# Reordering VectorE's queue in a fused mLSTM cell and gated feed-forward kernel

## The chip, the cores and the metric

The kernel runs on one core of a Trainium2 chip. A core has a matrix engine (TensorE, PE in the profile, its weight loads PEld), a vector engine (VectorE, DVE), an activation engine (ScalarE, ACT), a general engine (GpSimd, POOL) and a queue that here only issues transfers (SyncE, SP). Each engine works through its own instructions in order and waits on semaphores for the others. The metric is the device time of one execution in microseconds (us); less is better.

## The reference

For 4 batches, 8 heads, 768 steps and a head size of 40, an mLSTM cell is run step by step, its output becomes 3072 rows of 320, and a feed-forward block of width 2048 with the activation h * cos(h) follows:

```python
m_new = np.maximum(f_gate[:, :, t] + m, i_gate[:, :, t])
f_stab, i_stab = np.exp(f_gate[:, :, t] + m - m_new), np.exp(i_gate[:, :, t] - m_new)
C = f_stab[..., None, None] * C + i_stab[..., None, None] * np.einsum('bhd,bhe->bhde', vt, kt)
n = f_stab[..., None] * n + i_stab[..., None] * kt
denom = np.maximum(np.abs(np.einsum('bhd,bhd->bh', n, qt)[:, :, None]), 1.0)
y[:, :, t] = sigmoid(o_gate[:, :, t]) * np.einsum('bhde,bhe->bhd', C, qt) / denom
...
h = x @ w_in            # x: 3072 x 320, w_in: 320 x 2048
out = (h * np.cos(h)) @ w_out
```

w_in and w_out come as 64-bit floats and are made 32-bit on the chip.

## The kernel before, in words

**Chunks and periods.** The sequence is cut into 6 chunks c of 128 steps. One call of both_parts(c, b), called a *period* here, does the feed-forward of chunk c for a quarter of the width (two *slots*, each a pair of blocks of 128 columns of w_in for all four batches), and beside it the cell n = 4(c+1)+b, that is batch b of the next chunk. Chunk 5 has no cell beside it. first_cells does cells 0 to 3 ahead. Everything is emitted in one order written by hand (manual_schedule), and each engine's queue is that order cut down to its own instructions.

**A slot on the feed-forward side.** Up (L617) multiplies x by w_in into two PSUM tiles pup (L631 and L634, two buffers in all, so that the next Up waits until this one's are read). near (L639, ACT) rounds h to whole turns, rest (L642, DVE) forms the remainder, sin (L647, ACT) takes its sine, and gate (L654 in chunk 0, L659 in two halves after it, DVE) multiplies it with h: only the gate frees pup. sums (L723, POOL) forms sums of four blocks, and down or down_first (L727, L823, PE) multiply with w_out.

**The cell.** scores (L453, PE) writes ps. weigh (L459, DVE, two instructions) multiplies it into the decay matrix E in place and so frees ps. values_turned (L490 and L496, PE) writes hp into the PSUM buffers which ps had (pool ps_a has two), L496 with the weighed E. normalize_turned (L510 to L522, DVE) reads hp, fade (L577) decays the state, seam (L596, PE) makes the state's addition pu in a buffer that hp had, and state (L612, DVE) adds it. turn_blocks (L414) and turn_gates (L421, L425), on DVE, prepare the next cell. Cells below 7 (TURNED) use PE transposes and normalize instead.

**The decay matrix of the next cell** passes through three engines: decay_exponents subtracts on DVE (L375) and masks on POOL (L376), decay takes the exponential on ACT (L384). ACT changes its table for it and back for the sine (sin_next, L965), and then does the near of the second slot. On POOL the sums of the second slot stand behind the mask.

**Weights.** parts (ACT, L138 and L140) and join (DVE, L144, L146, L148, and an addition L149 on POOL, or on DVE where nc.vector is handed in) make 32-bit pieces. In chunk 0 a period makes three pieces of w_in for the next period (i=0 and i=1, 128x512, and w_in_l, 128x256) and two of w_out (128x640). The tiles wt and wm between parts and join have two buffers.

**Order of DVE in a period before.** First slot: rest, rest, weigh, in chunks 1 to 4 decay_exponents, gates; in chunk 0 the join of w_out and, after normalize, of w_in piece 1. Second slot: rest, rest, state, in chunk 0 the join of w_in piece 2, gates, in chunk 0 the join of w_in_l and of w_out, with turn_blocks and turn_gates between or after.

Of the kernel before, what the change touches and what calls it, by code (L numbers as in the profile page):

```python
# [29 lines left out]
def kernel(  # L30
# [20 lines left out]
    nc = tc.nc  # L51

    B, H, S, D = q.shape
# [16 lines left out]
    TURNED = 2 * B - 1  # L70
# [302 lines left out]
    def decay_exponents(n):  # L373
        E = Es[n]
        nc.vector.tensor_tensor(out=E, in0=E, in1=cols(n, 0, C), op=OP.subtract)  # L375
        nc.gpsimd.affine_select(out=E, in_=E, compare_op=OP.is_ge, fill=1.0e30, base=0,  # L376
                                pattern=[[0, H], [1, C]], channel_multiplier=-1)
# [461 lines left out]
    def first_cells():  # L839
        nc.vector.memset(nil, 0.0)  # L840
        gates_in()
        nc.scalar.copy(out=ident_b, in_=ident)
        load(0, "qk")
        later_gates_in()
        load(1, "qk")
        load(0, "v")
        load_o(0, (0, 1))
        load(2, "qk")
        load_E(0)
        load_E(1)  # L850
        warm(7)
        gates_first()
        later_fills()
        wall_in(0, 0, pmu)
        wall_in(0, 1, psum_o())
        spread(0, 0)
        gates_first_out()
        decay_exponents_half(0, 0)
        turn(0)
        turn_out(0, False)  # L860
        gates_sums()
        spread(0, 1)
        decay_exponents_half(0, 1)
        decay(0)
        weigh_k(0)
        load_E(2)
        load(1, "v")
        load(3, "qk")
        load(2, "v")
        load_E(3)  # L870
        load_o(0, (2, 3))
        load(3, "v")
        pieces.extend(weights_in(0))
        wall_in(1, 0, psum_o())
        wall_in(1, 1, psum_o())
        gates_less_sums()
        spread(1, 0)
        decay_exponents_half(1, 0)
        scores(0)
        gates_maxima()  # L880
        turn(1)
        weigh(0)
        turn_out(1, False)
        sigmoid(0, slice(0, 2))
        spread(1, 1)
        decay_exponents_half(1, 1)
        gates_exponents()
        decay(1)
        weigh_k(1)
        values(0)  # L890
        normalize(0)
        scores(1)
        turn(2)
        turn_out(2, False)
        warm(2)
        seam(0)
        weigh(1)
        seam_out(0)
        state(0)
        load_E(B)  # L900
        load(B, "qk")
        decay_exponents(2)
        decay(2)
        weigh_k(2)
        gates_exp()
        values(1)
        outs.append((0, weights_out(0)))
        load(B, "v")
        load_o(1, (0,))
        load_E(B + 1)  # L910
        normalize(1)
        scores(2)
        turn(3)
        seam(1)
        weigh(2)
        turn_out(3)
        seam_out(1)
        decay_exponents(3)
        gates_diagonal()
        values(2)  # L920
        decay(3)
        weigh_k(3)
        state(1)
        scores(3)
        weigh(3)
        pg = gates_turn()
        warm(5)
        values(3)
        join(*parts(*pieces.pop(0)))
        sigmoid(0, slice(2, 4))  # L930
        gates_keep(*pg)
        pieces.extend(weights_in(1))
        load(B + 1)
        outs.extend((p, weights_out(p)) for p in range(1, 3))
        load_o(1, (1, 2, 3))
        normalize(2)
        warm(5)
        seam(2)
        seam_out(2)
        second = parts(*pieces.pop(0))  # L940
        normalize(3)
        warm(4)
        seam(3)
        join(*second, nc.vector)
        decay_exponents(B)
        seam_out(3)
        join(*parts(*pieces.pop(0)), nc.vector)
        load_E(B + 2)
        state(2)
        state(3)  # L950

        nc.scalar.activation(out=spot, in_=spot, func=AF.Exp)
# [10 lines left out]
    def sin_next():  # L963

        nc.scalar.activation(out=spot, in_=spot, func=AF.Sin)  # L965
# [5 lines left out]
    def out_join(p, h, last=None):  # L971
        join(*h, last)
        if p + 3 < NF // 2:
            outs.append((p + 3, weights_out(p + 3)))

    def both_parts(c, b):

        n = (c + 1) * B + b
        cell = n < N
        begin = c == b == 0
        more = cell and n + 1 < N
        f2 = 2 * b
        slot = NF // 2 * c + f2
        sums(slot)
        up = Up(c, f2, cell_after_first if begin else None)
        if cell:
            scores(n)  # L990
            if begin:
                values_kept(n)

                warm(6, psum_o())
        for e in range(2):
            up.near(e)
        if begin:
            weigh(n)
        for e in range(2):
            up.rest(e)  # L1000
        if cell and not begin:
            weigh(n)
        if begin or more and c > 0:
            decay_exponents(n + 1)
        for e in range(2):
            up.sin(e)
            up.gate(e)
        if n == TURNED:
            turn_gates(n)
        if c == 0 and b == 1:  # L1010
            sigmoid(1, slice(1, B))
        if begin:
            sigmoid(1, slice(0, 1))
        h = ()
        if c == 0 and not begin:
            out_join(*out_parts())
        if pieces:
            h = parts(*pieces.pop(0))
        rests = []
        ends = any(step[2] == NP - 1 for step in plan.get(slot, ()))  # L1020
        if ends:
            rests = down(slot)
        if begin or more and c > 0:
            decay(n + 1)
        elif more:
            decay_by_bias(n + 1)
        if 0 < slot <= NP:
            down_first(slot - 1)
        elif slot and not ends:
            down(slot)  # L1030
        for rest in rests:
            rest()
        if cell:
            if n < TURNED:
                load(n + 2)
                if not begin:
                    values_kept(n)
                values(n)
                normalize(n)
                if h:  # L1040
                    join(*h)
            else:
                values_turned(n)
                if h:
                    join(*h)

                normalize_turned(n)
                if n + 2 < N:
                    load(n + 2, "q")
                last_in(n)  # L1050
                if n + 2 < N:
                    load(n + 2, "bkv")
            if TURNED <= n + 2 < N:
                load_G(n + 2)
            if n + 3 < N:
                load_E(n + 3)
            if b == B - 2 and c + 2 < NC:
                load_o(c + 2)
            fade(n)
            if n + 1 == TURNED:  # L1060
                turn_blocks(n + 1)
        h = ()
        sin_next()
        if pieces:
            h = parts(*pieces.pop(0))
        sums(slot + 1)
        up = Up(c, f2 + 1)
        if cell:
            seam(n)
        for e in range(2):  # L1070
            up.near(e)
        for e in range(2):
            up.rest(e)
        if cell and n < TURNED:
            seam_out(n)
        if cell:
            state(n)
        if h:
            join(*h)
        for e in range(2):  # L1080
            up.sin(e)
            up.gate(e)
        if b == B - 1 and 0 < c < NC - 2:
            sigmoid(c + 2)
            sin_next()
        if more:
            weigh_k(n + 1)
        if c == 1 and b < B - 1:
            two_differences(2 * b + 2)
        if pieces:  # L1090
            join(*parts(*pieces.pop(0)))
        if c == 0:
            down_first(f2)
        else:
            for rest in down(slot + 1):
                rest()
        if pieces:
            join(*parts(*pieces.pop(0)))
        if c == 0:
            if b + 2 < B:  # L1100
                pieces.extend(weights_in(b + 2))
            h = out_parts()
        if more and n + 1 < TURNED:
            turn(n + 1)
            turn_out(n + 1, c > 0)
        elif more and n + 1 > TURNED:
            turn_blocks(n + 1)
        if c == 0:
            out_join(*h)
            if b == B - 1:  # L1110
                more_units()
                two_differences(0)
                sigmoid(2)
                sin_next()
        if more and n + 1 > TURNED:
            turn_gates(n + 1)
# [43 lines left out]
```

## Time and profile before

| what | value |
|---|---|
| median of 5 runs | 535.59 us (533.8 to 539.48) |
| the profiled execution: its own time, its span | 535.59 us, 533.8 us |
| granted TensorE clock, mean | 0.997 |
| PE busy | 521.6 us (98%) |
| DVE busy | 397.3 us (74%) |
| ACT busy | 264.9 us (50%) |
| POOL busy | 209.8 us (39%) |

The span runs from the first to the last recorded instruction, and the time has 1.8 us around it. Chunk 0 begins at 37.6 us of the span, chunk 1 at 129.4, chunk 2 at 207.2, chunk 3 at 283.9, chunk 4 at 363.8 and chunk 5 at 442.6 (first Up of each). A timeline line gives start, duration, engine, line, operation and tiles, and in brackets the idle time before it with what ended it. A line of waits gives the total, the number and the longest.

### The profile page before, as it was taken

Reading aid. Unit: us, or ns where it says so; the run is one execution under the profiler, and the core shown is the slowest. Engines: PE = TensorE matmul, PEld = TensorE weight load, DVE = VectorE, ACT = ScalarE, POOL = GpSimd, SP = SyncE. Lnnn points to the kernel's source line nnn. Section 1 sums busy time; section 2 is a strip of 40 time slices with the busy share of each in tenths; the row PEclk is TensorE's granted clock in tenths of the full one; section 3 lists DMA queues with packets and bytes.
Section 4 is the critical chain, followed back from the end, with each engine's and each line's share of the span. In section 5 each row is a group of like instructions: output and inputs, shape, how many; then the busy total and the mean of one; then the engine's idle time right before and its main releaser. Section 6 shows DMA issues by size and latency. Waiting matters only on the chain.

```text
span 533.8 us, 10613 instructions
## 1 busy us (share of the span) xinstructions
PE 521.6 (98%) x3855; PEld 345.3 (65%) x3855; DVE 397.3 (74%) x864; ACT 264.9 (50%) x418; POOL 209.8 (39%) x409
## 2 busy tenths in 40 slices
PE   8999999999999999999999999999999999999996
PEld 6865566654565666556656567667567576657596
DVE  5779678889788887977988978968868854325253
ACT  4779696767633646552547353356354322313210
POOL 6423433333926531131531633533533425344350
PEclk9899999999999999999999999999999999999999
DMA  9999989822563365365266256266254100000000
GB/s 137 224 227 232 219 222 224 186 50 64 131 143 87 89 141 126 95 136 114 70 150 147 66 112 137 83 139 142 79 102 93 41 11 17 14 0 26 0 26 25
DMA packets 134860, 57.80 MB, mean 108 GB/s; under 512 B 70248, under 2 KB 130872, under 8 KB 134808
## 3 DMA queue, kind: packets, MB, share of 16 engines
q1 hardware_dynamic: 134664, 56.93, 48.2%
q8 instruction: 30, 0.49, 0.4%
q0 software_dynamic: 96, 0.18, 0.2%
q14 instruction: 22, 0.18, 0.1%
q10 hardware_dynamic: 48, 0.02, 0.0%
HBM read 50.76 MB, written 6.34 MB: 107 GB/s over the span
## 4 chain that ended last, share of the span: by engine, by line
PE 72%; DVE 12%; SPq 8%; DMA 3%; issue 2%; ACT 1%; POOL 1%; DVEq 0%; POOLq 0%; ACTq 0%
PE po L727 27%; PE pup L631 26%; PE pup L634 8%; PE po L823 4%; SPq L332 3%; PE ps L453 2%; PE hp L496 2%; DVE E L375 2%; DVE n L642 2%; DMA E<-M_d 1%; DVE wt L148 1%; PE hp L490 1%; DVE wt L146 1%; PE pu L596 1%; DVE E L459 1%
## 5 line engine op out<-in xcount | busy, mean ns | idle before, releaser
L631 PE MATMUL pup<-xT,w_in_sb 128*128 128x512 f32 x384 | 175.2, 599 | 3.6 <-DVE g L654 1.6
L639 ACT ACTIVATE n<-pup 128x512 int32<-128x512 f32 x96 | 52.0, 593 | 179.7 <-PE pup L634 179.7
L642 DVE SCALAR_TENSOR_TENSOR n<-pup,n 128x512 f32<-128x512 f32 x96 | 61.8, 686 | 91.0 <-ACT n L639 90.8
L631 PEld LDWEIGHTS pup<-xT,w_in_sb 128*128 128x128 f32 x384 | 69.6, 190 | 77.4 <-issue 63.4
L376 POOL TENSOR_SCALAR_AFFINE_SELECT E<-E 128x1024 f32<-128x1024 f32 x19 | 20.8, 1094 | 131.0 <-DVE E L375 125.1
L727 PE MATMUL po<-T,sg 128*128 128x160 f32 x426 | 69.5, 299 | 0.0
L647 ACT ACTIVATE n<-n 128x512 f32<-128x512 f32 x96 | 58.9, 630 | 16.1 <-DVE n L642 16.1
L727 PEld LDWEIGHTS po<-T,sg 128*128 128x128 f32 x426 | 61.7, 190 | 0.0
L723 POOL TENSOR_TENSOR sg<-g 128x128 f32<-128x128 f32 x66 | 30.2, 458 | 63.3 <-PE po L727 44.3
L634 PE MATMUL pup<-xT,w_in_l 64*128 64x512 f32 x192 | 54.2, 641 | 0.6 <-DVE w_in_l L149 0.6
L723 POOL TENSOR_TENSOR sg<-gg 128x128 f32<-128x128 f32 x66 | 30.2, 457 | 39.1 <-PE po L727 37.0
L634 PEld LDWEIGHTS pup<-xT,w_in_l 64*128 64x128 f32 x192 | 14.4, 184 | 37.0 <-issue 34.1
L727 PE MATMUL po<-w_out_sb,g 128*128 128x160 f32 (+1 forms) x180 | 38.3, 341 | 0.0
L823 PE MATMUL po<-w_out_sb,g 128*128 128x320 f32 x128 | 36.6, 439 | 0.5 <-POOL w_out_sb L149 0.4
L727 PEld LDWEIGHTS po<-w_out_sb,g 128*128 128x128 f32 x180 | 27.8, 189 | 11.0 <-issue 6.8
L414 DVE STREAM_TRANSPOSE t<-qs 128x512 f32<-128x512 f32 x34 | 34.9, 1105 | 0.0
L384 ACT ACTIVATE E<-E 128x1024 f32<-128x1024 f32 x21 | 22.2, 1058 | 25.3 <-POOL E L376 21.2
L727 PE MATMUL po<-w_out_sb,gg 128*128 128x160 f32 (+1 forms) x168 | 34.0, 329 | 0.0
L459 DVE TENSOR_TENSOR E<-ps,E 128x512 f32<-128x512 f32 x48 | 30.7, 680 | 2.5 <-ACT E L384 2.1
L453 PEld LDWEIGHTS ps<-t,t 40*128 40x128 f32 (+1 forms) x384 | 25.7, 192 | 9.7 <-issue 9.2
L659 DVE SCALAR_TENSOR_TENSOR g<-pup,n 128x256 f32<-128x256 f32 x82 | 30.6, 416 | 1.1 <-issue 0.6
L727 PE MATMUL po<-w_out_sb,sg 128*128 128x160 f32 x142 | 30.9, 299 | 0.0
(171 smaller groups left out, 852.5 us busy)
## 6 DMA issues: line engine op xcount, KB each, us to landing
E<-M_d SPq DMA_DIRECT2D x22, 512.0 KB
bits<-in_moe_w_in_dram SPq DMA_DIRECT2D x40, 128.0 KB
bits<-in_moe_w_out_dram SPq DMA_DIRECT2D x8, 640.0 KB
room<-G_d SPq DMA_DIRECT2D x34, 128.0 KB
ks<-in_k_dram SPq DMA_DIRECT2D x24, 160.0 KB
vs<-in_v_dram SPq DMA_DIRECT2D x24, 160.0 KB
out_dram<-o SPq DMA_DIRECT2D x18, 160.0 KB
o<-in_o_gate_dram SPq DMA_DIRECT2D x68, 40.0 KB
```

The source lines that it names most:

```text
L414: nc.vector.transpose(out=dst.rearrange("r p (t x) -> r p x t", x=T4), in_=src.rearrange("r p (x d) -> r p x d", x=T4)[:, :, :, 0:32])
L453: nc.tensor.matmul(ps[j][:, p], kT[r, p], qT[r, p], start=True, stop=True)
L459: nc.vector.tensor_tensor(out=w, in0=pss[n][j], in1=w, op=OP.mult)
L631: nc.tensor.matmul(pu, w_in_sb[:, i, ts(block(f2, e), 128)], x(i), start=(i == 0), stop=False)
L634: nc.tensor.matmul(pu, w_in_l[r, f2], x(NK, r), start=False, stop=True)
L639: nc.scalar.activation(out=self.n[e], in_=self.pu[e], func=AF.Copy, bias=0.25)
L642: nc.vector.scalar_tensor_tensor(out=self.n[e].bitcast(FP), in0=self.pu[e], scalar=0.25, in1=self.n[e], op0=OP.add, op1=OP.subtract)
L647: nc.scalar.activation(out=r, in_=r, func=AF.Sin, scale=TWO_PI_DOWN)
L659: nc.vector.scalar_tensor_tensor(out=gs[c, f2, s][:, ts(e, W)], in0=self.pu[e][:, ts(s, W)], scalar=TWO_PI, in1=n[:, ts(s, W)], op0=OP.mul ...
L723: engine.tensor_tensor(out=S[:, i], in0=x, in1=y, op=op)
L727: nc.tensor.matmul(out, g, w, start=start, stop=stop, skip_group_check=True)
L823: nc.tensor.matmul(po[0][b], gs[0, f // 2, f % 2][:, ts(b, C)], w_out_sb[:, f], start=(f == 0), stop=(f == NF - 1))
```

## The change

In chunks 1 to 4, one weigh moves between the two remainders of the first slot, decay_exponents of the next cell moves behind the gates, and in the second slot state moves behind the gates (from cell 7 on). In chunk 0, each period makes parts for w_in pieces 1 and 2 and joins both in its middle, ahead of the second slot's remainders; the join between state and the gates goes; fade moves ahead of these joins; the last join of w_out of each period ends on DVE instead of POOL; turn_blocks of cell 7 moves behind the gates. In first_cells the join of w_in_l and decay_exponents(4) change places. No instruction is added or removed but for the engine of four additions (128x640, L149).

```diff
@@ first_cells
         join(*second, nc.vector)
-        decay_exponents(B)
         seam_out(3)
         join(*parts(*pieces.pop(0)), nc.vector)
+        decay_exponents(B)
@@ both_parts
         if begin:
             weigh(n)
-        for e in range(2):
-            up.rest(e)
-        if cell and not begin:
+        up.rest(0)
+        if cell and c > 0:
             weigh(n)
-        if begin or more and c > 0:
+        up.rest(1)
+        if c == 0 and not begin:
+            weigh(n)
+        if begin:
             decay_exponents(n + 1)
         for e in range(2):
             up.sin(e)
             up.gate(e)
+        if more and c > 0:
+            decay_exponents(n + 1)
...
         if pieces:
-            h = parts(*pieces.pop(0))
+            h = [parts(*pieces.pop(0)) for _ in range(2 if begin else 1)]
...
                 values(n)
                 normalize(n)
-                if h:
-                    join(*h)
+                fade(n)
             else:
                 values_turned(n)
-                if h:
-                    join(*h)
+            if h:
+                if not begin:
+                    sin_next()
+                    h.append(parts(*pieces.pop(0)))
+                for piece in h:
+                    join(*piece)
+            if n >= TURNED:
...
-            fade(n)
-            if n + 1 == TURNED:
-                turn_blocks(n + 1)
-        h = ()
-        sin_next()
-        if pieces:
-            h = parts(*pieces.pop(0))
+            if n >= TURNED:
+                fade(n)
+        if begin or not h:
+            sin_next()
...
-        if cell:
+        if cell and n < TURNED:
             state(n)
-        if h:
-            join(*h)
         for e in range(2):
             up.sin(e)
             up.gate(e)
+        if n >= TURNED and cell:
+            state(n)
...
+        if n + 1 == TURNED:
+            turn_blocks(n + 1)
         if pieces:
             join(*parts(*pieces.pop(0)))
...
-        if pieces:
-            join(*parts(*pieces.pop(0)))
...
         if c == 0:
-            out_join(*h)
+            out_join(*h, nc.vector)
```

## The prediction

> **What bounds the kernel now.** I read the page's busy times first, then the waits of PE between 37 and 320 us, then the timeline of each engine over chunks 0 to 3.
>
> The busy times (us, share of the span, instructions):
>
> ```profile
> PE 521.6 (98%) x3855; PEld 345.3 (65%) x3855; DVE 397.3 (74%) x864; ACT 264.9 (50%) x418; POOL 209.8 (39%) x409
> ```
>
> PE sets the time. From the second period of chunk 3 on its timeline has no gap, so what other engines do there is worth nothing unless it becomes late. To be gained are PE's stalls before, and nothing more. Its waits (total us, number, longest):
>
> ```profile
> PE pup L631 <- DVE g L654: 1.6, 3, 0.6
> PE pup L631 <- DVE g L659: 0.9, 1, 0.9
> PE pup L634 <- DVE w_in_l L149: 0.6, 1, 0.6
> PE pu L596 <- DVE room L519: 0.5, 1, 0.5
> PE po L823 <- POOL w_out_sb L149: 0.4, 2, 0.2
> ```
>
> That is 4.0 us: mostly an Up that waits for gates, and pieces that are joined late. More hides in matmuls drawn long. PE in a chunk-1 period whose first slot has 16 w_out products of full width (L823, 4.5 us), and in one with 14 of half width (L727, 2.1 us):
>
> ```profile
> 139.40 0.67 PE L490 MATMUL hp<-room,st 40*32 40x128 f32 x32
> 141.01 3.70 PE L631 MATMUL pup<-xT,w_in_sb 128*128 128x512 f32 x8
> ...
> 157.87 0.94 PE L490 MATMUL hp<-room,st 40*32 40x128 f32 x32
> 159.95 3.70 PE L631 MATMUL pup<-xT,w_in_sb 128*128 128x512 f32 x8
> ```
>
> From hp's start to the next Up: 1.61 us in the first, 2.08 in the second. Seven periods are like the second (2.07 to 2.14). DVE says why:
>
> ```profile
> 155.61 1.29 DVE L642 SCALAR_TENSOR_TENSOR n<-pup,n 128x512 f32<-128x512 f32 x2 [2.17 <-ACT n L639]
> 156.82 1.28 DVE L459 TENSOR_TENSOR E<-ps,E 128x512 f32<-128x512 f32 x2
> 158.01 1.22 DVE L375 TENSOR_TENSOR E<-E,tab 128x1024 f32<-128x1024 f32 x1
> 159.14 1.41 DVE L659 SCALAR_TENSOR_TENSOR gg<-pup,n 128x256 f32<-128x256 f32 x4
> 160.47 0.51 DVE L510 STREAM_TRANSPOSE room<-hp 128x128 f32<-128x128 f32 x2
> ```
>
> hp is ready to start at 157.87, but the second weigh frees its buffer only at 158.10; the first gate's two halves end at about 159.9, where the Up starts. Weigh and gates are each late by less than a microsecond.
>
> **Chunks 1 to 4.** Let T be the start of the first remainder (155.61). Starts follow each other by 0.60 (L642, L459), 1.13 (L375) and 0.335 us (L659). New order: rest T, weigh T+0.60 and T+1.20, rest T+1.80. ACT's second sine (0.63 each) now starts after that, T+2.53 to T+3.16, so gate 0 runs T+2.40 to T+3.1 and gate 1 waits 0.13 and runs T+3.2 to T+3.9. L375 starts at T+3.87 (before T+2.40), L510 at T+5.0 (before T+4.86).
>
> Gain: the weigh ends 0.6 us earlier and gate 0 1.1 us earlier, more than the 0.5 us that PE loses there in all, so hp to Up becomes 1.61. In three periods of chunk 1 and two of chunk 2 (2.08, 2.13, 2.13, 2.14, 2.14) this gives 2.57. In the first periods of chunks 2 and 3 the half microsecond is lost again: PE then waits for L519 (at 221.74 and 298.88), which only gets later, by the 0.14 of L510; in chunk 3 also by POOL's later sums beside L521 to L577: I take -0.14 and -0.30. Bounds for the two together: 0 to -0.9 (three of those instructions stretched in each, as L577 was from 0.67 to 1.22 at 164.23).
>
> In the last period of chunk 2 the Up waits 0.9 at 283.87 for gates behind rest (281.15) and state (282.36). State goes behind them, 0.67. But ACT's near now ends its wait for the mask later: POOL's mask T+5.16, ACT's exponential T+6.3, table 1.28, dummy sine 0.2, near at 280.1 instead of 280.52 with PE 0.5 earlier. Up at 282.95 instead of 283.87, 0.92 of which 0.53 is counted above: 0.4 (0 to 0.6).
>
> The later mask is the new wait. Behind it on POOL stand the second slot's sums, 1.5 us later: at 240.0 rather than 238.5 for the first four against PE's use at 243.95, and in chunk 3 298.9 for the last four against about 302. Behind it on ACT stand the table, the dummy and near: 164.4 instead of 164.80, PE ready at about 164.15; DVE is not free before 165.9 in any case. State ends at 169.2; the scores that need its buffer start at 172.2. All hidden.
>
> **A rule against it.** POOL and DVE disturb each other:
>
> ```profile
> 120.81 1.24 DVE L512 SCALAR_TENSOR_TENSOR room<-room,least 128x8 f32<-128x8 f32 x1
> 122.09 1.01 DVE L513 SCALAR_TENSOR_TENSOR room<-room 128x8 f32<-128x8 f32 x1
> ```
>
> beside
>
> ```profile
> 120.50 1.53 POOL L149 TENSOR_TENSOR w_out_sb<-wt,wm 128x640 int32<-128x640 int32 x1 [6.79 <-ACT E L390]
> 121.98 1.09 POOL L391 TENSOR_SCALAR_AFFINE_SELECT E<-E 128x1024 f32<-128x1024 f32 x1
> ```
>
> Both end with the POOL instruction (L391 is the mask in chunk 0, of the same kind and length as L376); at 220.20 L512 took 0.17. The mask (1.09) used to lie under the gates, which read PSUM and kept their time; it now lies under L512 and moves everything up to L522 by 0.35 more. DVE's second remainders then start at 165.97 instead of 165.48, their gates at 167.2 against an Up at 168.7: hidden, and 1.4 us of DVE's 2.36 idle before the next period's remainder are left. The Trainium skill, "SBUF — State Buffer", Who interferes with whom, says that a DVE instruction with two SBUF inputs and a reading POOL instruction exclude each other for the whole instruction. By that rule L512 would be held for up to the whole mask, 1.09 per period, and by the rows for the 0.73 that is left of it at T+5.54. The gates' lead of 0.8 covers the 0.36 between them, so the sum is 3.97 by either.
>
> **Chunk 0.** (a) first_cells: w_in_l joined at 40.25 instead of 42.65 (the mask stretched its L146 to 1.08; its four steps unhindered, 0.33+0.3+0.43+0.43 from the nearest rows), so PE's 0.57 before L634 goes. Late next is weigh at 44.83, which stands behind the w_out join: that starts with ACT's L138 at 42.5 and meets kw on POOL. Gain 0.2 (-0.4 if kw holds a step for its 0.75, +0.4 if not). (b) Up at 60.78 and 107.93, each 0.63 idle, 0.80 late against the common step: the join between state and gates (0.43+0.43+0.69) goes, and w_in pieces come earlier. In the middle, the second join runs beside POOL's addition of the first (1.27) and takes about 2.5 instead of 1.6; fade (2 x 0.5 on POOL), now ahead of these additions, meets normalize's last steps and may cost up to 0.5 more, which is in the ends below. At 60.78 DVE had 2.55 idle there: gates at 58.1 instead of 59.95, PE ready at 59.9, gain 0.8. PE's wait for w_out at 66.62 (0.14 over the common step) goes, since DVE adds it in about 0.83 (0.69 x 640/512, L149 at 38.09) and not 1.54. (c) At 84.50 nothing was lost; rest moves from 79.90 to 81.3, gates stay at 83.2 to 84.4: 0. (d) At 107.93 DVE had no idle time. Gates at 106.3, so the Up starts at 107.13, but turn_blocks (2.1) now stands between the gates and the join of w_in_l, whose POOL addition ends at 111.1 to 111.6; L634 wants it at 110.6 and started at 111.53 before. Of 0.8, plus 0.28 for w_out at 113.77, I keep 0.3 (-0.1 to 1.1: the two ends of that join). Each w_out addition (0.83) on DVE ends before the next remainder, which had 1.29, 1.43, 1.29 and 0.85 idle.
>
> ACT's order: at the start of chunk 0 the second parts (1.2) go ahead of the exponential, same sum before near. The weights' transfers land early enough (4096-byte packets of w_in end at 44, 70 and 90 us against uses after 50, 78 and 99); SP issues in the same order.
>
> **Sum.** 2.57 - 0.44 + 0.4 + 0.2 + 0.8 + 0.14 + 0.3 = 3.97. The profiled execution took 535.59, which is also the median of the five runs: 535.59 - 4.0 = **531.6 us**, 0.7% less. Adding the low ends (five hp periods 1.8, -0.9, 0, -0.4, 0.6 for (b), -0.1) gives 1.0, the high ends (2.6, 0, 0.6, 0.4, 0.94, 1.1) 5.6: 530.0 to 534.6.
>
> **Rivals.** (1) All stalls go and DVE isn't held by POOL: high ends, and the waits at L596 (298.88) and 49.10 (0.5 each) too: 6.6, 529.0. For it: PE's remaining stalls are that small. Against: L519 gets later in my order. (2) The stalls go but come back at the next DVE wait (L634, L596, L519), or hp waits for turn_gates and not weigh: only (b) and 0.1 to 0.5 remain, 534.5. (3) Slower: the mask's place. If mask, exponential and two tables take over 1.8 us longer than I lay out (1.0 of DVE's own lateness and 0.8 of the gates' lead), the second slot's gates hold the Up in up to 15 periods; at 2.5 us it is 15 x 0.7 = 10.5, less 4: 542. Against: the chain's parts are measured (1.09, 1.06, 1.28, 0.2) and POOL is idle before the mask.
>
> **How the numbers follow.** A change of under about 1% can't be told from none in this kernel. Forecast 0.55, rival 1 0.20, rival 2 0.15, rival 3 0.10. Faster by over 1% is below 530.2: rival 1 and a little of the forecast, 0.23. Slower by over 1% (above 540.9): 0.08 of rival 3. Within 1%: 0.69. Range 528.8 to 536.5: it takes in the bounds, rival 2, most of rival 1 and rival 3's mild end.
>
> **What would show it.** L490's 32 at 0.67 and 1.61 from hp to Up in all periods of chunks 1 to 3; no wait before the second period's Up (60.78); a longer wait at L596 in the first periods of chunks 2 and 3; L512 near 0.7 under the mask; L634 near 111 waiting for POOL's w_in_l. Wrong if PE waits for g L659 in second slots (rival 3), or if L490 keeps 0.94.

## The result and the profile after

The changed kernel took 533.72 us (median of 45 executions, 531.69 to 536.76) against 534.6 (87 executions, 532.54 to 539.59) for the kernel before: a ratio of 0.998, 95% interval 0.9967 to 0.9993. That is 0.9 us where 4.0 were predicted. The profiled execution took 534.12 us, its span is 532.4. One execution of experiment 5 below, 661.22 us long at a mean granted clock of 0.751, is left out of its ratio.

The busy times after:

```profile
PE 519.2 (98%) x3855; PEld 343.4 (64%) x3855; DVE 409.3 (77%) x868; ACT 264.0 (50%) x418; POOL 204.9 (38%) x405
```

PE is 2.4 us less busy than in the profile before. Its waits between 37 and 320 us (total us, number, longest), the same view as in the prediction:

```profile
PE pt L434 <- issue: 1.9, 1, 1.9
PE pu L596 <- DVE room L519: 1.3, 2, 0.7
PE pup L631 <- DVE g L659: 1.2, 1, 1.2
PE pup L631 <- DVE g L654: 0.9, 1, 0.9
PE pup L634 <- POOL w_in_l L149: 0.7, 1, 0.7
PE pt L434 <- ACT xT L604: 0.4, 1, 0.4
PE po L823 <- DVE w_out_sb L149: 0.2, 1, 0.2
```

That is 6.6 us of waits. Before, it was 4.2 us: the prediction's list leaves out 0.2 at L631 for xT (L604). The two longest, at L434 and L596, are new or longer. Yet the part that was planned in chunk 1 is there: PE and DVE in the period that the prediction showed from 155.61 on.

```profile
158.38 0.67 PE L490 MATMUL hp<-room,st 40*32 40x128 f32 x32
158.98 1.08 PE L496 MATMUL hp<-E,vs 128*32 128x128 f32 x32
159.99 3.70 PE L631 MATMUL pup<-xT,w_in_sb 128*128 128x512 f32 x8
```

```profile
156.73 1.28 DVE L459 TENSOR_TENSOR E<-ps,E 128x512 f32<-128x512 f32 x2
157.92 0.68 DVE L642 SCALAR_TENSOR_TENSOR n<-pup,n 128x512 f32<-128x512 f32 x1
158.52 1.54 DVE L659 SCALAR_TENSOR_TENSOR gg<-pup,n 128x256 f32<-128x256 f32 x4
159.97 1.22 DVE L375 TENSOR_TENSOR E<-E,tab 128x1024 f32<-128x1024 f32 x1
161.10 0.51 DVE L510 STREAM_TRANSPOSE room<-hp 128x128 f32<-128x128 f32 x2
161.65 0.73 DVE L512 SCALAR_TENSOR_TENSOR room<-room,least 128x8 f32<-128x8 f32 x1
```

L490's 32 products take 0.67, hp to Up is 1.61 (both so in every period of chunks 1 to 3), the second weigh ends ahead of the second remainder, and L512 takes 0.73 under the mask: each as predicted.

**Where the time went in chunk 0.** The start of every group of PE's instructions, after minus before, gives the shift by place. PE enters chunk 0 3.2 us early for a reason that is no part of the change: the page's line of the clock, 40 slices of 13.3 us, before and then after.

```profile
PEclk9899999999999999999999999999999999999999
```

```profile
PEclk9999998999999999999999999999999999999999
```

In the profile before, the granted clock was 0.5 from 16.27 to 19.68, in the first cells. After, it was 0.5 from 82.99 to 86.40. Each window lasted 3.413 us. The 3.2 us lead grows to 4.4 us by 74.8 and is gone at 88.3, 1.7 us of it to the halved clock. The chain of work that ended last says why (start, us, what):

```profile
62.05 2.28 SPq L129
...
65.30 5.32 DMA bits<-in_moe_w_in_dram
...
70.72 0.68 ACT wt L138
```

The same piece on ACT before:

```profile
71.70 0.70 ACT L138 ACTIVATE wt<-bits 128x512 f32<-128x512 f32 x1
```

ACT's, DVE's and PE's timelines there (after):

```profile
66.87 0.79 ACT L140 ACTIVATE wm<-bits 128x640 int32<-128x640 uint32 x1
70.72 0.68 ACT L138 ACTIVATE wt<-bits 128x512 f32<-128x512 f32 x1 [3.07 <-DMA bits<-in_moe_w_in_dram]
```

```profile
77.83 0.43 DVE L144 TENSOR_SCALAR wt<-wt 128x512 f32<-128x512 f32 x1 [4.26 <-ACT wt L138]
...
80.31 1.28 DVE L642 SCALAR_TENSOR_TENSOR n<-pup,n 128x512 f32<-128x512 f32 x2
81.51 0.67 DVE L612 TENSOR_TENSOR st<-st,pu 40x164 f32<-40x164 f32 x2
```

```profile
82.28 0.63 PE L434 MATMUL pt<-ident,ks 128*128 128x128 f32 x4 [1.89 <-issue]
83.05 5.34 PE L631 MATMUL pup<-xT,w_in_sb 128*128 128x512 f32 x8
```

A w_in piece that is issued from 62.05 lands at 70.6; ACT has been waiting for it for 3.07 us. Behind it on ACT stand the exponentials, a table and the second piece's parts; behind those on DVE the second join, remainders and state; and behind state PE, whose second pt takes over the PSUM buffer of pu (the profile names no releaser for this wait; the pool has two buffers). The eight L631 then take 5.34 instead of 3.7 us, since the clock is halved just there.

### The profile page after: what moved, and what is told of

Its sections match the earlier page's. It is cut to its first block, busy times and chain, and to the rows that moved or that the text cites. A ratio compares the mean times of both kernels' runs of the same rounds, so it can differ in the third digit from the quotient of the medians.

```text
span 532.4 us, 10606 instructions
## 1 busy us (share of the span) xinstructions
PE 519.2 (98%) x3855; PEld 343.4 (64%) x3855; DVE 409.3 (77%) x868; ACT 264.0 (50%) x418; POOL 204.9 (38%) x405
## 4 chain that ended last, share of the span: by engine, by line
PE 76%; DVE 10%; SPq 5%; ACT 4%; DMA 2%; issue 2%; POOL 0%; DVEq 0%; ACTq 0%; POOLq 0%
PE po L727 28%; PE pup L631 27%; PE pup L634 8%; PE po L823 3%; PE hp L496 3%; SPq L332 2%; PE ps L453 2%; DMA bits<-in_moe_w_in_dram 2%; PE hp L490 2%; DVE n L642 1%; PE pu L596 1%; DVE wt L146 1%; DVE E L459 1%; DVE E L375 1%; SPq L129 1%
## 5 line engine op out<-in xcount | busy, mean ns | idle before, releaser
L631 PE MATMUL pup<-xT,w_in_sb 128*128 128x512 f32 x384 | 177.1, 604 | 2.5 <-DVE g L659 1.2
L642 DVE SCALAR_TENSOR_TENSOR n<-pup,n 128x512 f32<-128x512 f32 x96 | 63.2, 686 | 74.1 <-ACT n L639 73.7
L631 PEld LDWEIGHTS pup<-xT,w_in_sb 128*128 128x128 f32 x384 | 70.2, 191 | 77.1 <-issue 64.3
L727 PE MATMUL po<-T,sg 128*128 128x160 f32 x426 | 69.4, 299 | 0.0
L727 PEld LDWEIGHTS po<-T,sg 128*128 128x128 f32 x426 | 61.7, 190 | 0.0
L634 PE MATMUL pup<-xT,w_in_l 64*128 64x512 f32 x192 | 54.6, 641 | 0.7 <-POOL w_in_l L149 0.7
L634 PEld LDWEIGHTS pup<-xT,w_in_l 64*128 64x128 f32 x192 | 14.7, 184 | 37.3 <-issue 34.9
L727 PE MATMUL po<-w_out_sb,g 128*128 128x160 f32 (+1 forms) x180 | 38.3, 341 | 0.0
L823 PE MATMUL po<-w_out_sb,g 128*128 128x320 f32 x128 | 36.6, 439 | 0.2 <-DVE w_out_sb L149 0.2
L727 PEld LDWEIGHTS po<-w_out_sb,g 128*128 128x128 f32 x180 | 27.8, 189 | 11.0 <-issue 6.8
L727 PE MATMUL po<-w_out_sb,gg 128*128 128x160 f32 (+1 forms) x168 | 34.0, 329 | 0.0
L453 PEld LDWEIGHTS ps<-t,t 40*128 40x128 f32 (+1 forms) x384 | 25.4, 188 | 9.5 <-issue 9.0
L659 DVE SCALAR_TENSOR_TENSOR gg<-pup,n 128x256 f32<-128x256 f32 x78 | 29.9, 418 | 2.1 <-ACT n L647 1.2
```

Of the source, the lines that this page charges most:

```text
L453: nc.tensor.matmul(ps[j][:, p], kT[r, p], qT[r, p], start=True, stop=True)
L631: nc.tensor.matmul(pu, w_in_sb[:, i, ts(block(f2, e), 128)], x(i), start=(i == 0), stop=False)
L634: nc.tensor.matmul(pu, w_in_l[r, f2], x(NK, r), start=False, stop=True)
L642: nc.vector.scalar_tensor_tensor(out=self.n[e].bitcast(FP), in0=self.pu[e], scalar=0.25, in1=self.n[e], op0=OP.add, op1=OP.subtract)
L659: nc.vector.scalar_tensor_tensor(out=gs[c, f2, s][:, ts(e, W)], in0=self.pu[e][:, ts(s, W)], scalar=TWO_PI, in1=n[:, ts(s, W)], op0=OP.mul ...
L727: nc.tensor.matmul(out, g, w, start=start, stop=stop, skip_group_check=True)
```

## The experiments

Two theories for this place. H1: the transfers of w_in set the pace of chunk 0, and a lead on PE is lost to them. H2: the second join, now ahead of remainders and state on VectorE, holds these up. Theory A is the reading of the stages: chunks 1 to 3 gain 2.1 us (1.8 when the small steps are counted too), chunk 0 loses. (The Up at 83.05 is the first of chunk 0's third period; some expectations call it the second period's second.)

Beside the medians, executions are compared by their mean granted clock: one of 0.998 or more is taken to have no half-clock window of 3.413 us in it (such a window takes 0.003 off the mean), one of 0.994 to 0.997 is taken to have one. Of 104 executions of the kernel before beside these experiments, 69 had none (median 534.13), 20 had one (535.56), and 15 had more than one (539.5). Of 46 of the changed kernel only four had none (532.78, from 531.69 to 533.57), 35 had one (533.70), and seven had more (536.6). The experiments ran in four rounds (1 to 4, 5 to 8, 9 to 11, and 12), in which the kernel before without a window took 534.15, 534.47, 533.88 and 533.96: a difference between kernels of two rounds is uncertain by about half a microsecond.

**1. Chunks 1 to 4 alone.** The kernel before, with

```diff
-        for e in range(2):
-            up.rest(e)
-        if cell and not begin:
+        up.rest(0)
+        if cell and c > 0:
             weigh(n)
-        if begin or more and c > 0:
+        up.rest(1)
+        if c == 0 and not begin:
+            weigh(n)
+        if begin:
             decay_exponents(n + 1)
...
+        if more and c > 0:
+            decay_exponents(n + 1)
...
-        if cell:
+        if cell and n < TURNED:
             state(n)
...
+        if n >= TURNED and cell:
+            state(n)
```

> The kernel before with the reorder of chunks 1 to 4 alone (weigh between remainders, decay_exponents and state behind gates). Theory A (the trace of after read by stages: chunks 1 to 3 gain 2.1 us, chunk 0 keeps none of what it gains and loses about as much again): this half alone is worth 2.1 us, a ratio of 0.996 to the kernel before, faster than the whole change. Rival (the gain of chunks 1 to 4 depends on chunk 0's new order, or the two profiles differ there by chance): ratio 0.998 to 1.000. In the profile by theory A: hp to the next Up 1.61 us in all periods of chunks 1 to 3, and waits at L596 of about 1.3 us.

533.09 us, ratio 0.9972 (0.9941 to 1.0003); without a window 532.65, so 1.5 less than before. The half alone is as good as the whole. Its profile had no half-clock window, so PE was 3 us early in chunk 0 in the old order too, and 0.86 of this was lost at the same place (82.42). ACT's waits between 40 and 130 us:

```profile
ACT wt L138 <- DMA bits<-in_moe_w_in_dram: 1.5, 2, 1.0
```

The profile before had no such wait.

**2. Chunk 0 alone.** The changed kernel with the order of chunks 1 to 4 put back (the edit above undone).

> The changed kernel with the order of chunks 1 to 4 put back, so that the change of chunk 0 stands alone. The prediction had 1.4 us of gain for it (ratio 0.997). Theory A: it loses 0.3 to 1.2 us (ratio 1.0005 to 1.002), since the lead of up to 4.4 us that PE has before the second period is gone by that period's second Up. If the difference of the half-clock window between the two profiles accounts for part of the shift, about 1.000.

535.0 us, ratio 1.0005 (0.9985 to 1.0025); all 12 executions had a half-clock window. In the profiled one it came at 35.07, PE reached chunk 0 as late as in the profile before, and the loss at the Up of 84.50 was only 0.27: with PE late, the transfers are nearly in time (ACT waits 0.19 for the piece), and the prediction's zero for it nearly holds.

**3. Early transfers.** The changed kernel, with

```diff
         slot = NF // 2 * c + f2
+        if c == 0 and b + 2 < B:
+            coming = weights_in(b + 2)
+            pieces.extend(next(coming) for _ in range(2))
...
-                pieces.extend(weights_in(b + 2))
+                pieces.extend(coming)
```

> The changed kernel with the transfers of the first two w_in pieces for the next period but one issued at the start of each period of chunk 0 and not at its end. Theory H1 (ACT waits for these transfers, 3.07 us idle ahead of its L138 at 70.72, and everything up to the Up at 83.05 follows): that wait goes, the second period's second Up starts 1.5 to 2.5 us earlier against its cell's start, and the time falls by 1 to 2.5 us (ratio to the changed kernel 0.995 to 0.998). Theory H2 (the second join, standing ahead of remainders and state on DVE, is what delays): DVE still does 2.5 us of join there, the second Up gains 0.5 at most, ratio 0.999 to 1.000. If the E and q, k, v transfers now come too late instead, slower than the changed kernel.

529.77 us, ratio to before 0.9911 (0.9878 to 0.9944): 4 us less than the changed kernel. ACT and PE at the place (start, us):

```profile
67.74 0.67 ACT L138 ACTIVATE wt<-bits 128x512 f32<-128x512 f32 x1
```

```profile
79.81 0.60 PE L434 MATMUL pt<-ident,ks 128*128 128x128 f32 x4
80.24 3.65 PE L631 MATMUL pup<-xT,w_in_sb 128*128 128x512 f32 x8
```

ACT doesn't wait, PE neither, and the Up starts 2.8 us earlier and runs at full clock. The second join is still there (74.86 to 77.5). H1 holds; H2 isn't needed.

**4. The second join late.** The changed kernel, in the second and third period with

```diff
-        h = ()
+        h, late = (), ()
...
+                late = [] if begin else [h.pop()]
...
+        for piece in late:
+            join(*piece)
+        if pieces:
+            join(*parts(*pieces.pop(0)))
         if n + 1 == TURNED:
             turn_blocks(n + 1)
-        if pieces:
-            join(*parts(*pieces.pop(0)))
```

> The changed kernel with the second w_in piece of the second and third period joined behind the second slot's gates again (its parts stay in the middle), turn_blocks behind the joins. Theory H2: remainders start when near is ready (78.9 and not 80.3 in the second period), state and gates 1.4 us earlier, Up at 81.6 instead of 83.05; ratio to the changed kernel 0.997 to 0.998. Theory H1: the pieces of ACT are late anyway (L138 at 70.72 and what follows it), ratio 0.9995 to 1.000. In the fourth period w_in_l is joined earlier than after turn_blocks: L634 there no longer waits (0.7).

533.78 us, ratio to before 0.9985 (0.9959 to 1.001), the same as the changed kernel: H2's 1.4 us didn't come. The wait for w_in_l went, but a wait of 1.3 at L823 for w_out came in its place. The profiled execution had half-clock windows at 16.7 and from 30.3 to 40.6, so its place at 80 can't be read. By itself this run doesn't settle H2, since the new wait is about as long as the gain that H2 promised; experiment 3 does.

**5. Early transfers in the kernel before.** The edit of 3 in the kernel before (without the second join behind the gates, which in the old order found no piece left; so too in 8).

> The kernel before with the transfers of the first two w_in pieces issued one period earlier, and nothing else. Theory H1 in its narrow form (the changed order needs these transfers 6 us earlier than the old one, which hardly waited for them: 0 to 1.5 us of ACT waits): 0 to 1.0 us less than the kernel before, ratio 0.998 to 1.000. Rival (early transfers are worth 4 us in any order): ratio 0.992.

532.82 us, ratio 0.997 (0.9941 to 0.9999); without a window 532.44 against 534.13: 1.7 us. The kernel before lost time to these transfers too, about half of the 3.3 that the changed one lost (532.78 to 529.48).

**6. Filling TensorE's idle time.** The changed kernel, between the two turns of cell 6, with

```diff
+                for i in range(14):
+                    nc.tensor.matmul(po[0][i % B].rearrange("p (a x) -> p a x", x=64), nil,
+                                     nil[:, 0:64].unsqueeze(1).to_broadcast([128, 5, 64]), start=False, stop=False)
```

> The changed kernel with 14 products of zeros (about 0.14 us each) added to the sums of w_out where TensorE stands idle for 1.9 us ahead of the second turn at 82.28. If it is TensorE's idleness in the 3.413 us before 82.99 (busy 0.38 of it) that brings the half clock of 82.99 to 86.40: granted clock 1.0 there, 8 L631 in 3.68 instead of 5.34 us, time less by about 1.7 us (ratio to the changed kernel 0.997), with no stall removed. If the half-clock window comes by chance, or moves to another place: ratio 0.999 to 1.003, the products costing what they last.

536.65 us, ratio to before 1.0036 (1.0011 to 1.0061): 2.9 slower than the changed kernel, and 10 of 12 executions still had a window. The profiled one had it at 16.12, so PE was late at 82 and not idle there: the products only cost their 2.06 us. It doesn't say whether idleness brings the window.

**7. Two waits mended.** The kernel of 3, with

```diff
-        if begin:
+        early = more and c == 2 and b == B - 1
+        if begin or early:
             decay_exponents(n + 1)
...
-        if more and c > 0:
+        if more and c > 0 and not early:
             decay_exponents(n + 1)
...
+        if pieces:
+            join(*parts(*pieces.pop(0)))
         if n + 1 == TURNED:
             turn_blocks(n + 1)
-        if pieces:
-            join(*parts(*pieces.pop(0)))
```

> The kernel with early transfers, with two more edits: in chunk 0's last period w_in_l is joined ahead of turn_blocks, and in the last period of chunk 2 decay_exponents stands ahead of the gates as before. If the two waits seen in the changed kernel (0.7 at L634 for w_in_l, 1.2 at an L631 of chunk 2 for the gate) come from these two places: both go below 0.2, and the time falls by 0.5 to 1.5 us against the kernel with early transfers alone. If what is gained is lost at the next wait (L596 in the first periods of chunks 2 and 3, 1.7 together): within 0.3 us of it.

530.07 us, ratio to before 0.9909 (0.9879 to 0.9939); without a window 528.74 against 529.48 in 3. L634 starts 0.74 earlier against its surroundings, but w_out is then 0.35 late. At the end of chunk 2 the Up behind the second slot's gates gains 0.71, and the Up behind the first slot's gates, which now wait for L375, loses 0.53; with 0.41 lost and 0.41 gained after it (L727, L596), the edit there is worth 0.2.

**8. Early transfers with chunk 0's old order.** The kernel of 1 with the edit of 3.

> The reorder of chunks 1 to 4 and the early transfers, with chunk 0's order on VectorE as before. It tells what chunk 0's new order is worth once transfers are out of the way: the prediction's terms for it sum to 1.4 us, and the steps between the two traces without the Up at 82.42 sum to 1.3, so 531.1 here against 529.8 with it. Rival (the early transfers do it all, and chunk 0's order adds nothing): 529.8 here too.

532.28 us, ratio to before 0.9939 (0.9913 to 0.9964); without a window 530.64. So chunk 0's new order is worth 1.16 (to 529.48) once the transfers are early.

**9. Idleness put in.** The kernel of 3, with

```diff
+        if c == 0 and b == 1:
+            for _ in range(3):
+                nc.vector.tensor_tensor(out=rooms[3][0:BH], in0=rooms[3][0:BH], in1=rooms[3][0:BH], op=OP.mult)
         if cell and n < TURNED:
             state(n)
```

> The kernel with early transfers, and three products of 32x768 on VectorE (about 0.9 us each) ahead of the second period's state, which make TensorE wait about 2.3 us for the second turn at 79.8, as it did in the changed kernel, with no transfer late. If TensorE's idleness alone brings a half-clock window of 3.413 us behind it: nearly every execution has a granted clock of 0.997 or less, the window lies at about 80 to 86 us in the profile, and the loss is 2.8 + 1.7 = 4.5 us, to about 534. If the window had another cause (transfers, chance): 2.8 us, to about 532.5, with the clock at 0.998 or more in about half of the executions, as without the dummies.

534.91 us, ratio to before 1.0006 (0.9971 to 1.0041): 5.1 more than the kernel of 3, and 11 of 12 executions had a window. So far this is what was expected if idleness brings the window. But the profile contradicts the place:

```profile
84.31 0.63 PE L434 MATMUL pt<-ident,ks 128*128 128x128 f32 x4 [2.50 <-issue]
85.08 3.67 PE L631 MATMUL pup<-xT,w_in_sb 128*128 128x512 f32 x8
```

PE was idle for 2.5 us and the Up behind it ran at full clock. This execution had its one window at 46.21.

**10. turn_blocks last.** The kernel of 3, with turn_blocks of cell 7 behind both joins:

```diff
-        if n + 1 == TURNED:
-            turn_blocks(n + 1)
         if pieces:
             join(*parts(*pieces.pop(0)))
...
             out_join(*h, nc.vector)
+            if n + 1 == TURNED:
+                turn_blocks(n + 1)
```

> The kernel with early transfers, turn_blocks of cell 7 behind the joins of w_in_l and of w_out. If the two waits in chunk 0's last two periods (0.7 at L634 for w_in_l, 0.2 to 0.5 for w_out) come from turn_blocks standing ahead: both go, 0.7 to 1.0 us less than with early transfers alone (529.8 to about 529.0). If scores of cell 7 now wait for turn_blocks, or the lead goes at the next wait: within 0.3.

532.22 us, ratio to before 0.9954 (0.9922 to 0.9986): 2.4 worse than the kernel of 3. PE's waits:

```profile
PE ps L453 <- DVE t L414: 1.9, 1, 1.9
```

The two waits are gone, but scores now wait for the blocks, and the half-clock window came right there (110.17).

**11. Early transfers and chunk 0 alone.** The kernel of 2 with the edit of 3.

> Chunk 0's new order and the early transfers, with chunks 1 to 4 as before. Against the kernel before with early transfers (532.8) it tells once more what chunk 0's order is worth when transfers are not late: the prediction's terms say 1.4 less (531.4), and against the kernel with everything (529.8) what chunks 1 to 4 are worth: 2.1 by the traces (531.9), 2.5 by the prediction (532.3). If chunk 0's order is worth nothing even then: 532.8.

531.47 us, ratio to before 0.9938 (0.9908 to 0.9969); without a window 531.29: 1.15 less than 5, and 1.81 more than 3.

**12. A better version.** The kernel of 3, w_in_l ahead of turn_blocks as in 7, and in chunk 0's first period

```diff
-        if begin:
-            decay_exponents(n + 1)
         for e in range(2):
             up.sin(e)
             up.gate(e)
-        if more and c > 0:
+        if begin or more and c > 0:
             decay_exponents(n + 1)
```

> The kernel with early transfers, w_in_l joined ahead of turn_blocks, and in chunk 0's first period decay_exponents behind the gates. The gates of that period then run 1.13 us earlier, so the Up at 46.0 no longer waits (0.86), and chunk 0's first term (w_in_l 0.64 earlier) is no longer given back; the join of w_in_l takes 0.7 off L634 and gives 0.35 back at w_out. Sum 0.86 + 0.39 = 1.2 less than with early transfers alone: 528.3 where no half-clock window occurs (529.5 without the two edits), about 530.5 with one. If the leads are lost at the next wait: 529.5.

528.71 us (528.54 to 530.23), ratio to before 0.9877 (0.9827 to 0.9927), the fastest here; none of its six executions had a half-clock window. PE in the first period, in the kernel of 3 and then in this one:

```profile
46.00 3.70 PE L631 MATMUL pup<-xT,w_in_sb 128*128 128x512 f32 x8 [0.86 <-DVE g L654]
```

```profile
45.00 3.70 PE L631 MATMUL pup<-xT,w_in_sb 128*128 128x512 f32 x8
```

The Up's wait is gone, but 0.54 of it comes back at the second period's first Up. With 0.4 gained at w_in_l and w_out that makes 0.7 us by the two traces; without a window the times differ by 0.8.

## Why the prediction was wrong

**The step that failed** is "The weights' transfers land early enough (4096-byte packets of w_in end at 44, 70 and 90 us against uses after 50, 78 and 99)", and with it the zero of (c), "At 84.50 nothing was lost". The use that counts is ACT's L138 on the first piece of a period. In the profile before it started at 71.70, 1.4 us after that piece had landed (70.33 by its semaphores), and on the next period's piece at 93.05; the 78 and 99 of the prediction fit L138 on the second pieces (78.17 and 99.47). The sum's own terms ahead of that place (0.2 + 0.8 + 0.14) move it forward by 1.14, most of those 1.4. And that execution had a half-clock window in its first cells: PE came into chunk 0 at 37.59, and at 34.3 to 34.8 in the profiles that had none there (1, 3, 5 and after among them), so the profile showed the transfers with 3 us more slack than most executions give them (69 of 104 had no window). Experiments 2 and 3 show both sides: with PE late, the loss at that Up is 0.27; with the transfers early it is gone, and 3.3 us with it.

**Chunk 0's own terms were nearly right.** With early transfers its order is worth 1.15 us (5 against 11, 532.44 to 531.29) and 1.16 (8 against 3), where the terms sum to 1.44. The two pairs ran in different rounds; set against its round's own kernel before, the order is worth 0.56 and 0.84. The steps between the traces, which don't depend on the rounds, sum to 1.17 in both pairs. (b) came at 60.78 with the 0.80 predicted, and 0.29 at w_out instead of 0.14. (a): L634 gained 0.64, and 0.56 was given back at the period's second Up, to the gates behind weigh, as named; in 12, with L375 moved behind these gates, that Up waits no more, and half of the gain is kept to the next. (d) was wrong in sign: 0.49 gained at the Up and 0.06 at w_out, 0.74 lost again at L634 to POOL's w_in_l, the wait that the prediction named and priced too low. About 0.2 is lost, where its worst end was 0.1 lost. POOL's addition after:

```profile
111.02 0.84 POOL L149 TENSOR_TENSOR w_in_l<-wt,wm 128x256 int32<-128x256 int32 x1 [3.96 <-DVE wt L148]
```

**Chunks 1 to 4** are worth 1.80 (5 against 8) and 1.81 (11 against 3), where 2.53 was predicted; by the shift between traces it is 1.77 (before and after) and 1.97 and 1.78 (the two pairs). The five hp periods give 2.58 in the traces (2.57 predicted). The first period of chunk 2 loses 0.13 (0.14 predicted), that of chunk 3 gains 0.31 (0.30 lost predicted), since PE came there later. Small steps at Ups and L634 of chunk 1 and after take 0.3. The 0.4 of the last period of chunk 2 failed: the Up behind its second slot lost 0.27, and 0.42 more went behind it, where L634 and L453 took 1.55 and 1.48 instead of 1.13 and 1.06 (for what, wasn't tried). In 1, 3 and 8 that 0.42 isn't lost, but L596 in the first period of chunk 3 then loses 0.54 to 0.56 and not 0.15. The prediction had ACT's near as the last wait there; near started at 278.80 and was done in time, and DVE was not free. In that period L512 took 0.79 beside the mask (0.43 before) and L521 0.91 beside POOL's kw (0.43 before):

```profile
278.12 0.91 DVE L521 TENSOR_TENSOR room<-room,room 128x256 f32<-128x256 f32 x1
```

Kw's place behind the later mask was not in this term. The second slot's remainder starts at T+10.0; the prediction's shifts of 0.14 and 0.35 alone would have put it at about T+9.5 (DVE was free at T+9.0 before).

**What remains of the sum.** Without a window the change is worth 1.35 us (534.13 to 532.78, the latter from four executions): 1.15 + 1.8 less the 1.6 by which late transfers hold the new order more than the old. And the half-clock window is more frequent after it, 42 of 46 executions against 35 of 104, which takes about 0.5 of it back and leaves the 0.9 measured. That the window became more frequent is counted; why it did is not settled. In kernels in which PE stands idle for some 2 us in chunk 0 (after, 2, 4, 9, 10, as far as their profiles or their orders say) 10 of 94 executions were without one, in before, 1, 3, 5, 7, 8, 11 and 12 it was 115 of 176. These groups were formed after the results were seen. In 9 the window of the profiled execution didn't follow the idle stretch, and 6, which was to fill that stretch, kept its windows.

The measured 533.72 lies between the sum's low and high ends (530.0 to 534.6), but that is luck: the sum starts from 535.59, the median of five executions and 1.0 above that of 87, and of its 4.0 us only 0.9 came. All the signs named under "What would show it" came as well. They tested the terms of the sum, and none of them tested the term that was put at nothing.

**The rivals.** None named a transfer. Rival 2, "The stalls go but come back at the next DVE wait", has the nearest time (534.5), but not for its reason: (b) and the hp periods kept their gains. Rival 3 didn't happen: no second slot's gates hold the Up in chunks 1 to 3 but those at the end of chunk 2 (1.17, and 0.90 before). The Trainium skill's rule ("SBUF — State Buffer", Who interferes with whom) agrees with the size that the rows gave: L512 started at 161.65 beside a mask that ran from 161.26 to 162.35, and took 0.73, the rest of the mask and not its whole 1.09.

## What to carry to other kernels

When a change makes an engine ask for transferred data earlier, find the first instruction that reads the data, on the engine that reads it, and compare its start with the landing. Take off all the lead that the change itself brings, and the lead that an undisturbed start brings. A profile without a wait for a transfer only says that this one execution wasn't early enough to meet it. Gains in several stages add up only as far as no shared supply sets the pace: here the order on VectorE paid (3 us) once the transfers' order was changed with it. Before a difference of 1 us is read from two profiles, see where each had its clock halved.

## What was not expected of the hardware

The half-clock window. In 10 of 14 profiles the granted clock fell to 0.5 once for 3.413 us (in experiment 4 a second time, for 10.24), apart from the very end; in each profile the starts lie in a grid of 3.413 us that is not tied to the kernel's start. By PE's instructions, the stretch of 3.413 us ahead of the first was busy 0.38 (after), 0.40 (7), 0.43 (2), 0.44 (10), 0.63 to 0.66 (6, before and 8), 0.72 (4) and 0.75 (9 and 11, beside products with 41 or 82 columns). The one of 10.24 in 4 came behind a stretch that was busy 0.91. After the first such window later stretches at 0.43 (9) to 0.74 (before) were not followed by one; in 1 and 3, which had none, neither were stretches at 0.66 around 280 us (so it isn't the first alone). So the busy share alone doesn't tell when a window comes. The same code pays it in one execution and not in the next; that this goes by where the grid falls is a guess. 12, with the 0.86 of idle time around 45 taken out, had none in six. The Trainium skill ("TensorE: Matmul & The Clock Gate", Part 1: The HAM clock gate) states a free-running window of 3413 ns and half the clock after an idle one; the length and the grid agree, but here windows came behind stretches that were 0.38 to 0.75 busy and not idle.
